# Attention backward of a transformer block: dQ by 256-column matmuls over two column strips of TensorE in place of 128-column matmuls over four

## The chip, the cores and the metric

The kernel runs on one core of a Trainium2 chip. The metric is the device time of one execution in microseconds (us), lower is better. Within the core the engines work side by side and meet at semaphores: TensorE (PE, with PEld for its weight loads), VectorE (DVE), ScalarE (ACT), GpSimd (POOL) and SyncE (SP), which issues most of the DMAs.

## What is computed

The reference is one block with adaptive layer norm: x + ga * attention(h1), then x + gb * mlp(h2), and its vector-Jacobian product for all inputs. There are 2048 tokens, width 512, 32 heads of 16 columns. The change lies in the gradient of the attention:

```python
qkv = (x @ wqkv).reshape(B, S, 3, H, Dh)          # H = 32, Dh = 16
scores = einsum('bhqd,bhkd->bhqk', q, k) * scale  # scale = Dh ** -0.5
p = softmax(scores)
o = einsum('bhqk,bhkd->bhqd', p, v)
# backward: P = exp(scores) normalized, dP = dO V^T - rowsum, dS = P * dP
# dQ = scale * dS K,  dK = scale * dS^T Q,  dV = P^T dO
```

Weights and activations are bf16 and sums are kept in float32.

## The kernel before

The kernel is a sequence of stages: QKV and the forward attention with the MLP woven in, the MLP's backward, the attention's backward (`attn_bwd`, from some 1184 to 2414 us of the profile), and the gradients of the QKV projection. In the attention's backward the order on PE and SP is the program order (`manual_schedule`), and in the forward part and the last stage too; ScalarE's, VectorE's and GpSimd's orders follow from it.

`attn_bwd` loops over 8 groups `g` of four heads, two pairs `jp` of heads in each, 4 blocks `c` of 512 keys, and 16 blocks `ib` of 128 queries taken in fours (`ib0`, `i`). One pass of the innermost loop handles 128 queries, 512 keys and two heads `a`. 8 x 2 x 4 x 16 makes 1024 passes. In a pass:

- For each head, PE multiplies Q by K into a tile `st` of PSUM (L1584; three such buffers), then ScalarE takes the exponential into `pu` (L1587).
- Between the two, PE makes dP of the pass before into `dp` (L1509; three buffers), and VectorE multiplies it with `pu` into `ds` (L1513). S uses one half of the array's rows and dP the other. In one pass of eight (`off`) the second of these products is made by GpSimd (L1522), from a copy that ScalarE makes (L1521).
- After an odd pass, `kv_two` calls `kv` for two older query blocks: 4 matmuls each (L1455), 512 columns over four strips of 32 columns of the array, that add dK and dV into `acckv`. When all queries of a key block are done, ScalarE copies it to `kvT` (L1458).
- After an even pass, four units of `dq` (eight if many are queued) add dQ into `accq` (L1478). A unit is one head `a`, one 128-key part `sub` of the key block and the four query blocks of an `ib0`. Its operand `dsT` holds the transposed `ds`.
- In pass `i == 2` a DMA or, for a part in every second four, PE transposes `ds` into `dsT` (`turn_ds`, L1543, and ScalarE's copy L1544). The DMA is issued on SP at the end of the four (`dS`, L1530), into one of four `dsT` buffers.
- After all key blocks of a pair, VectorE scales `accq` into `dqT` (L1483). `turn_q` transposes this on PE (L1491) and ScalarE writes the token-major result `dq_t` (L1492). For dK and dV `turn` does the same (L1468, L1472). Turns are taken from a queue at `i == 1`, which is directly after the dQ matmuls of the pass before.

`accq` is one bank of PSUM (128 partitions x 512 float32). Before the change its partition strip is the query block within the four, `i`, and its column block is `b = ib0 // 4`.

Of the kernel before, what the change touches and what calls it, by code (L numbers as in the profile page):

```python
# [10 lines left out]
F32 = mybir.dt.float32  # L11
ACT = mybir.ActivationFunctionType
ALU = mybir.AluOpType
# [6 lines left out]
P = 128  # L20
DH = 16
# [84 lines left out]
class K:  # L106
# [1322 lines left out]
    def attn_bwd(self):  # L1429
# [7 lines left out]
        tc, nc = self.tc, self.nc  # L1437
        S, D, H, NQ, ST, SC = self.S, self.D, self.H, self.NQ, self.ST, self.SC
        G = 4
        W = 4 * DH  # L1440
        dtp, kvp, stp, dpp = self.dtp, self.kvp, self.stp, self.dpp
        accp = self.accp
        acckv = accp.tile([P, 512], F32, name="acckv")
        nc.vector.memset(acckv[:], 0.0)
        accq = accp.tile([P, ST // G, P], F32, name="accq")
        masked, kvs = self.masked, self.kvs
        pend, pendq, turnq = [], [], []

# [11 lines left out]
        def turn(g, jp, kvT, s0):  # L1460

            if kvT is None:
                return turn_q(g, jp)
            h0 = 4 * g + 2 * jp
            n = ST // 2
            tp = stp.tile([P, n, P], BF16, name="st")
            for st in range(n):
                nc.tensor.transpose(tp[:, st, :], kvT[:, (s0 + st) * P:(s0 + st + 1) * P], self.ident[:])  # L1468
            v = tp[:].rearrange("p s (t a e) -> p t s a e", t=2, a=2)
            for t, dst in enumerate((self.dk_t, self.dv_t)):  # L1470
                d = dst[:, s0:s0 + n, h0 * DH:(h0 + 2) * DH].rearrange("p s (a d) -> p s a d", a=2)
                nc.scalar.copy(d, v[:, t, :, :, 0:DH])  # L1472

        def dq(u):
            (T, g, jp, c, ib0, a, sub, dsT) = u
            col = 32 * (2 * jp + a) - DH * a
            for i in range(G):
                nc.tensor.matmul(accq[32 * i:32 * i + 32, ib0 // G, :], lhsT=T["K"][:, 4 * c + sub, col:col + 32],  # L1478
                                 rhs=dsT[:, (i * 2 + a) * 4 + sub, :],
                                 start=(c == 0 and ib0 == 0 and a == 0 and sub == 0), stop=False,  # L1480
                                 skip_group_check=True)
            if (c, ib0, a, sub) == (SC - 1, ST - G, 1, 3):
                nc.vector.tensor_scalar(self.dqT[:], accq[:].rearrange("p b q -> p (b q)"), self.scale, None, ALU.mult)  # L1483
                turnq.append((g, jp, None, 0))

        def turn_q(g, jp):

            h0 = 4 * g + 2 * jp
            tp = stp.tile([P, ST // G, P], BF16, name="st")
            for b in range(ST // G):  # L1490
                nc.tensor.transpose(tp[:, b, :], self.dqT[:, b * P:(b + 1) * P], self.ident[:])  # L1491
            nc.scalar.copy(self.dq_t[:, :, h0 * DH:(h0 + 2) * DH], tp[:].rearrange("p b (i e) -> p (b i) e", i=G))  # L1492

        def kv_two(n=2):
            for u in pend[2 - n:2]:
# [51 lines left out]
        T = self.T0  # L1547
        last = None
        for g in range(NQ):
            for jp in range(2):  # L1550
# [15 lines left out]
                for c in range(SC):  # L1566
                    c0 = 512 * c
                    for ib0 in range(0, ST, G):
# [6 lines left out]
                        for i in range(G):  # L1575
                            ib = ib0 + i
                            q = slice(ib * P, (ib + 1) * P)
                            if turnq and i == 1:
                                turn(*turnq.pop(0))
                            pu = self.pup.tile([P, 2, 512], BF16, name="pu")  # L1580
                            for a in range(2):
                                stt = stp.tile([P, 512], F32, name="st")
                                rs = slice(64 * jp, 64 * jp + 64)
                                nc.tensor.matmul(stt[:], lhsT=T["QT"][rs, q], rhs=masked["KT"][a][rs, c0:c0 + 512],  # L1584
                                                 start=True, stop=True)
                                held = dP(last, a) if last else None
                                nc.scalar.activation(pu[:, a, :], stt[:], ACT.Exp, scale=self.scale)  # L1587
                                if held is not None:
                                    dP_pool(last, held)
                            if last:  # L1590
                                dS(last)
                            last = (T, g, jp, c, ib, kvT, pu, dsg, i, grp)
                            if i % 2 == 1 and len(pend) >= 4:
                                kv_two()
                            elif i % 2 == 0 and len(pendq) > 4 * G:
                                for _ in range(8 if len(pendq) > 6 * G else 4):
                                    dq(pendq.pop(0))
                            if i == 2:
                                turn_ds(dsg, grp, off(c, ib))
            T = Tn  # L1600
        with tc.manual_schedule(engines=ALL):
            for t in (2, 0):
                for p in self.wq_pieces(t):
                    nc.gpsimd.dma_start(*p)
            for a in range(2):
                dP(last, a)
            dS(last)
            while len(pend) > 2:
                kv_two()
            kv(pend[0])  # L1610
            for _ in range(2 * G):
                dq(pendq.pop(0))
            kv_two(1)
            k0, v0, k1 = [dpp.tile([P, 512], F32, name="dp") for _ in range(3)]
            self.dw_mm(k0, 1, 0, 0, ST // 2)
            turn(*turnq.pop(0))
            for _ in range(2 * G):
                dq(pendq.pop(0))
            self.dw_mm(v0, 2, 0, 0, ST // 2)
            self.dw_mm(k0, 1, 0, ST // 2, ST)  # L1620
            self.col_sum(1)
            self.dw_mm(v0, 2, 0, ST // 2, ST)
            self.col_sum(2)
            self.cs_bc(1)
            while pendq:
                dq(pendq.pop(0))
            self.cs_bc(2)
            turn(*turnq.pop(0))
            self.dw_mm(k1, 1, 1, 0, ST)
# [312 lines left out]
```

## Time and profile before

| what | value |
|---|---|
| median of 3 runs | 2524.97 us (2520.79 to 2530.05) |
| profiled execution | 2524.31 us, its span 2522.4 us |
| granted TensorE clock | 0.998 |
| dQ matmuls (L1478) | 8192, 128 x 32 weights, 128 columns, median 219 ns each as recorded |
| dK and dV matmuls (L1455) | 4096, 128 x 16 weights, 512 columns, 381 ns each |
| S (L1584) and dP (L1509) matmuls | 2048 each, 512 columns, 381 and 382 ns |
| exponentials (L1587) | 2048, 641 ns each |
| products ds (L1513) | 1920, 681 ns each |
| transposes of ds by DMA (L1530) | 256, median 7.1 us from issue to landing |

A matmul's recorded duration is its way through the array and is longer than the time until the next may start, so starts must be compared, not durations. The same holds for ACTIVATE and TENSOR_TENSOR: one starts before the record of the one before it ends. In a line of groups the columns are the line of the code, the engine, the operation, what it writes and reads, shape, count, busy time and mean. In the timeline they are the start, the length of the merged group, engine, line, operation and count.

### The profile page before, as it was taken

Reading aid. Unit: us, or ns where it says so; the run is one execution under the profiler, and the core shown is the slowest. Engines: PE = TensorE matmul, PEld = TensorE weight load, DVE = VectorE, ACT = ScalarE, POOL = GpSimd, SP = SyncE. Lnnn points to the kernel's source line nnn. Section 1 sums busy time; section 2 is a strip of 40 time slices with the busy share of each in tenths; the row PEclk is TensorE's granted clock in tenths of the full one; section 3 lists DMA queues with packets and bytes.
Section 4 is the critical chain, followed back from the end, with each engine's and each line's share of the span. In section 5 each row is a group of like instructions: output and inputs, shape, how many; then the busy total and the mean of one; then the engine's idle time right before and its main releaser. Section 6 shows DMA issues by size and latency. Waiting matters only on the chain.

```text
span 2522.4 us, 76903 instructions
## 1 busy us (share of the span) xinstructions
PE 2433.1 (96%) x30791; PEld 1107.9 (44%) x30791; DVE 1705.4 (68%) x3519; ACT 2296.2 (91%) x3773; POOL 713.9 (28%) x1289
## 2 busy tenths in 40 slices
PE   8999999999999999989999999999999999999998
PEld 4555555555555554673333333333333333333343
DVE  6222223422332343667999999999999999999957
ACT  7999999999999997535999999999999999999945
POOL 2344531321131022255222222222222222222223
PEclk9999999999999999999999999999999999999999
DMA  4589761441343044699999999999999999999997
GB/s 167 134 178 202 179 114 64 116 99 44 103 118 74 24 137 129 139 191 214 234 221 218 218 226 220 223 227 218 219 218 223 225 221 221 222 228 226 237 211 198
DMA packets 1260558, 446.30 MB, mean 177 GB/s; under 512 B 1204052, under 2 KB 1228246, under 8 KB 1260198
## 3 DMA queue, kind: packets, MB, share of 16 engines
q1 hardware_dynamic: 1219654, 336.29, 70.7%
q0 software_dynamic: 38464, 104.04, 13.9%
q8 instruction: 241, 3.95, 0.7%
q10 hardware_dynamic: 2080, 1.05, 0.1%
q14 instruction: 119, 0.97, 0.1%
HBM read 75.83 MB, written 64.49 MB: 56 GB/s over the span
## 4 chain that ended last, share of the span: by engine, by line
PE 59%; ACT 22%; DMA 11%; issue 4%; DVE 3%; SPq 1%; POOL 0%; DVEq 0%; ACTq 0%; POOLq 0%
ACT pu L391 18%; PE st L1584 17%; DMA dsT<-ds 8%; PE acckv L1455 8%; PE st L388 8%; PE accq L1478 5%; PE accbank L322 3%; PE dp L1509 3%; ACT pu L1587 2%; PE dps L1050 2%; PE pps L1237 2%; PE dps L995 1%; DVE ds L1513 1%; PE st L1543 1%; PE pps L631 1%
## 5 line engine op out<-in xcount | busy, mean ns | idle before, releaser
L1513 DVE TENSOR_TENSOR ds<-dp,pu 128x512 bf16<-128x512 f32 x1920 | 1178.3, 681 | 44.5 <-PE dp L1509 26.4
L1587 ACT ACTIVATE pu<-st 128x512 bf16<-128x512 f32 x2048 | 1073.9, 641 | 39.4 <-PE st L1584 21.3
L391 ACT ACTIVATE pu<-st 128x1024 bf16<-128x1024 f32 x992 | 912.2, 1077 | 5.4 <-PE st L388 5.1
L388 PE MATMUL st<-QTm,KTq 128*128 128x512 bf16 x1984 | 588.4, 377 | 19.7 <-ACT pu L391 6.1
L322 PEld LDWEIGHTS <-pu 128*128 128x128 bf16 x8192 | 347.2, 96 | 236.2 <-issue 3.2
L322 PE MATMUL accbank<-Vaug,pu 128*128 128x17 bf16 x8192 | 357.6, 171 | 1.2 <-ACT Vaug L522 0.9
L1509 PE MATMUL dp<-kvm,q 64*128 64x512 bf16 x1024 | 356.4, 382 | 2.2 <-DVE g2w L1056 0.7
L1509 PE MATMUL dp<-kvm,dOTg 64*128 64x512 bf16 x1024 | 356.2, 382 | 0.9
L1584 PE MATMUL st<-kvm,QTg 64*128 64x512 bf16 x1024 | 327.2, 381 | 10.5 <-ACT pu L1587 7.4
L1584 PE MATMUL st<-kvm,q 64*128 64x512 bf16 x1024 | 326.6, 380 | 10.8 <-ACT pu L1587 7.6
L388 PEld LDWEIGHTS <-KTq 128*128 128x128 bf16 x1984 | 188.2, 96 | 177.5 <-issue 125.9
L1522 POOL TENSOR_TENSOR ds<-junk,pu 128x512 bf16<-128x512 f32 x64 | 73.7, 1151 | 378.6 <-DVE ds L1513 336.7
L1522 POOL TENSOR_TENSOR ds<-csq,pu 128x512 bf16<-128x512 f32 x64 | 73.8, 1154 | 356.6 <-ACT csq L1521 356.6
L302 POOL DMA_DIRECT2D QTm<-QTq_d x124 | 63.5, 514 | 342.7 <-PE st L388 321.3
L1455 PE MATMUL acckv<-ds,Qg 128*16 128x512 bf16 x1024 | 154.3, 381 | 0.0
L1455 PE MATMUL acckv<-pu,dOg 128*16 128x512 bf16 x1024 | 154.2, 381 | 0.0
L1455 PE MATMUL acckv<-pu,q 128*16 128x512 bf16 x1024 | 154.0, 381 | 0.0
L1455 PE MATMUL acckv<-ds,q 128*16 128x512 bf16 x1024 | 154.0, 381 | 0.0
L329 DVE RECIPROCAL rl<-accbank 128x4 f32<-128x4 f32 x128 | 22.9, 179 | 159.5 <-PE accbank L322 159.2
L1584 PEld LDWEIGHTS <-q 64*128 64x128 bf16 x1024 | 58.1, 94 | 137.9 <-issue 104.5
L1584 PEld LDWEIGHTS <-QTg 64*128 64x128 bf16 x1024 | 57.7, 94 | 137.7 <-issue 102.7
L1509 PEld LDWEIGHTS <-q 64*128 64x128 bf16 x1024 | 88.4, 93 | 64.2 <-issue 47.4
(387 smaller groups left out, 3138.6 us busy)
## 6 DMA issues: line engine op xcount, KB each, us to landing
KTq<-KTq_d POOLq DMA_DIRECT2D x24, 512.0 KB, 3.8
duT_d<-auT POOLq DMA_DIRECT2D x3, 1792.0 KB, 8.2
aT_d<-rT POOLq DMA_DIRECT2D x3, 1792.0 KB, 11.6
KTq_d<-KTq SPq DMA_DIRECT2D x32, 128.0 KB, 2.0
QTq_d<-ev_fm SPq DMA_DIRECT2D x32, 128.0 KB, 3.4
ktm_d<-ev_tm POOLq DMA_DIRECT2D x32, 128.0 KB, 2.5
VTq_d<-vT POOLq DMA_DIRECT2D x4, 1024.0 KB, 5.8
dsT<-ds SPq DMA_TRANSPOSE x256, 7.1
```

Source lines behind the costliest of these rows:

```text
L302: nc.gpsimd.dma_start(QTm[j][32 * j:32 * j + 32, :], self.QTq_d[g, 32 * j:32 * j + 32, 512 * qc:512 * (qc + 1)])
L322: nc.tensor.matmul(acc[:, a, sub, :], lhsT=pu[:, a, sub * P:(sub + 1) * P], rhs=Vaug[:, kb, h, :], start=(kb == 0 and a == 0 and sub == 0) ...
L388: nc.tensor.matmul(stt[:, a, :], lhsT=KT[:, kb * P:(kb + 1) * P], rhs=QTm[2 * jp + a][:], start=True, stop=True)
L391: nc.scalar.activation(pu[:], stt[:], ACT.Exp, scale=self.scale)
L1050: nc.tensor.matmul(pt[:], lhsT=a[st], rhs=g_tm[:, st, :], start=(st == 0), stop=(st == ST - 1))
L1455: nc.tensor.matmul(acckv[r:r + DH, :], lhsT=T[n][:, ib, col:col + DH], rhs=src[:, a, :], start=(ib == 0), stop=(ib == ST - 1))
L1478: nc.tensor.matmul(accq[32 * i:32 * i + 32, ib0 // G, :], lhsT=T["K"][:, 4 * c + sub, col:col + 32], rhs=dsT[:, (i * 2 + a) * 4 + sub, :], ...
L1509: nc.tensor.matmul(dp[:], lhsT=T["dOT"][rd, ib * P:(ib + 1) * P], rhs=masked["VT"][a][rd, 512 * c:512 * (c + 1)], start=True, stop=True)
L1513: nc.vector.tensor_tensor(dsg[:, i, a], dp[:], pu[:, a, :], ALU.mult)
L1522: nc.gpsimd.tensor_tensor(dsg[:, i, 1], f[:], pu[:, 1, :], ALU.mult)
L1584: nc.tensor.matmul(stt[:], lhsT=T["QT"][rs, q], rhs=masked["KT"][a][rs, c0:c0 + 512], start=True, stop=True)
L1587: nc.scalar.activation(pu[:, a, :], stt[:], ACT.Exp, scale=self.scale)
```

## The change

A unit of `dq` issues two matmuls of 256 columns in place of four of 128. `h` picks two neighbouring query blocks of the four; they lie 8 blocks of 128 apart in `dsT`, so the moving operand has two runs of 128 columns. Each `h` has a strip of 32 array columns of its own, strips 0 and 1 for even `b`, 2 and 3 for odd `b`, and half of the bank's columns. The sum lands in another place of `accq`, so `turn_q`'s copy is written as two copies of half the width, which undo it. The transposes between, the scaling and all loads stay.

```diff
-        accq = accp.tile([P, ST // G, P], F32, name="accq")
+        accq = accp.tile([P, 512], F32, name="accq")
...
-            for i in range(G):
-                nc.tensor.matmul(accq[32 * i:32 * i + 32, ib0 // G, :], lhsT=T["K"][:, 4 * c + sub, col:col + 32],
-                                 rhs=dsT[:, (i * 2 + a) * 4 + sub, :],
-                                 start=(c == 0 and ib0 == 0 and a == 0 and sub == 0), stop=False,
+            b = ib0 // G
+            for h in range(2):
+                r, o = 32 * (2 * (b % 2) + h), 256 * (b // 2)
+                nc.tensor.matmul(accq[r:r + 32, o:o + 256], lhsT=T["K"][:, 4 * c + sub, col:col + 32],
+                                 rhs=dsT[:].rearrange("p (i w) k -> p i w k", i=G)[:, 2 * h:2 * h + 2, 4 * a + sub, :],
+                                 start=(c == 0 and b < 2 and a == 0 and sub == 0), stop=False,
                                  skip_group_check=True)
...
-                nc.vector.tensor_scalar(self.dqT[:], accq[:].rearrange("p b q -> p (b q)"), self.scale, None, ALU.mult)
+                nc.vector.tensor_scalar(self.dqT[:], accq[:], self.scale, None, ALU.mult)
...
-            nc.scalar.copy(self.dq_t[:, :, h0 * DH:(h0 + 2) * DH], tp[:].rearrange("p b (i e) -> p (b i) e", i=G))
+            for h in range(2):
+                nc.scalar.copy(self.dq_t[:, 8 * h:8 * h + 8, h0 * DH:(h0 + 2) * DH].rearrange("p (s i) e -> p s i e", i=2),
+                               tp[:, 2 * h:2 * h + 2, :].rearrange("p i (s e) -> p s i e", s=G))
```

## The prediction, made before the changed kernel was run

> **What bounds the kernel now.** I read the page's parts 1 and 4 first, then the busy times by stage, then TensorE's timeline inside the changed stage. The page says that PE and ScalarE are both near full over the span, and that the chain that ended last is mostly PE's:
>
> ```profile
> PE 2433.1 (96%) x30791; PEld 1107.9 (44%) x30791; DVE 1705.4 (68%) x3519; ACT 2296.2 (91%) x3773; POOL 713.9 (28%) x1289
> ...
> PE 59%; ACT 22%; DMA 11%; issue 4%; DVE 3%; SPq 1%; POOL 0%; DVEq 0%; ACTq 0%; POOLq 0%
> ```
>
> The changed matmuls (L1478) run from 1183.9 to 2414 us. Busy times by stage (the second line is the attention backward; columns are length, PE, PEld, DVE, ACT, POOL, clock, DMA):
>
> ```profile
> 0.00:1184.00 1184.00, 1142.53 (x13162) 645.06 (x13166) 450.40 (x1400) 1046.78 (x1246) 362.81 (x596) 1.00 0.53 127
> 1184.00:2414.00 1230.00, 1192.95 (x17184) 419.57 (x17187) 1173.43 (x1915) 1196.49 (x2423) 316.78 (x633) 1.00 1.17 223
> ```
>
> In that stage PE, VectorE and ScalarE are all 95 to 97% busy, so no one busy share names the bound. PE's timeline shows who waits:
>
> ```profile
> 1606.91 0.39 PE L1584 MATMUL st<-kvm,q 64*128 64x512 bf16 x1
> 1606.91 0.39 PE L1509 MATMUL dp<-kvm,q 64*128 64x512 bf16 x1
> 1607.14 0.38 PE L1584 MATMUL st<-kvm,q 64*128 64x512 bf16 x1
> 1607.14 0.38 PE L1509 MATMUL dp<-kvm,q 64*128 64x512 bf16 x1
> 1607.45 0.41 PE L1478 MATMUL accq<-dsT,keep 128*32 128x128 bf16 x16
> 1607.79 0.39 PE L1584 MATMUL st<-kvm,q 64*128 64x512 bf16 x1
> 1607.79 0.39 PE L1509 MATMUL dp<-kvm,q 64*128 64x512 bf16 x1
> 1608.01 0.38 PE L1584 MATMUL st<-kvm,q 64*128 64x512 bf16 x1
> 1608.30 0.37 PE L1509 MATMUL dp<-kvm,q 64*128 64x512 bf16 x1
> 1608.60 0.39 PE L1455 MATMUL acckv<-ds,q 128*16 128x512 bf16 x2
> ```
>
> I call one pass over a query block a step: S0, P0, S1, P1 (scores L1584, and dP L1509 of the step before), then a burst: dQ (16 matmuls) in even steps, dK/dV (L1455, 8 matmuls) in odd ones. Where nothing waits, S and P start together (1607.14). At 1608.30 P1 starts 0.29 us after its S1: it waits for a dp bank that VectorE (L1513) still reads. So PE, although "busy", waits here.
>
> The start stamps of the trace give the sums. Over the 1230 us, PE's shortest steps are 226+3+303+339 = 871 ns with a dQ burst and 226+3+303+541 = 1073 with a dK/dV burst; 512 of each are 995 us, 128 blocks of transposes (L1543, 329 ns) 42, and 48 turns (L1468, L1491, 330 to 550) some 24: 1061. VectorE starts a tile every 598 ns when fed: 1920 + 16 are 1158. ScalarE: 2048 x 477, 256 copies x 465, 64 x 569, 64 x 262, 16 x 482 are 1157. Hence VectorE and ScalarE set the pace, PE has 169 us of waits, and the 72 us above 1158 are starts that VectorE missed.
>
> **What the Trainium skill says.** "TensorE: Matmul & The Clock Gate", section on the back-to-back issue gap, gives 134 cycles at 128 columns and 262 at 256, at 2.4 GHz 56 and 109 ns. The trace agrees for the first: groups of four dQ matmuls start 56 ns apart. The 256 is in no trace yet; 512 columns (L1455) repeat after 219. The same page, on packing small matmuls, says that matmuls in different column groups overlap with starts about 4 ns apart; here 2 to 3 ns. Its section on LDWEIGHTS prices a load by its columns, P/1.2: an estimate of 27 ns for 32. In the trace these loads are issued ahead and hide. "TensorEngine Tiling (Array Packing)", key properties, says that a change of tiling mode drains the array. The trace agrees: from the last dQ start to the next S 148 ns pass, not 56. The change keeps 128x32 tiles and the number of switches.
>
> **The change part by part.** All times below stand against the profiled execution, 2524.31 us (span 2522.4, 1.9 around it), 0.03% under the median 2524.97.
>
> Burst. A unit was four matmuls of 128 columns over four strips, 56 ns. It becomes two of 256 over two strips; four units in a row have the same block of queries, so they use the same two strips, and the other two stand idle. A unit takes 109 ns. Four units: 3 x 53 more between starts, 53 more in the last, some 6 less for fewer starts: 339 becomes 543, +204. The dK/dV burst is the check: 2 x 512 columns, as many as 4 x 256, take 541. Ends: with one load of 27 ns exposed per unit, +312; if instructions rather than columns cost, -112 (rival 3). I take +205. 512 bursts make 105 us on PE, whose sum becomes 1166: level with VectorE's 1158, and no more than 8 us above. What the end sees is how much of each 205 PE's lead covers.
>
> Regular steps. VectorE starts tile n at 598n; a dp bank can be rewritten 728 ns after that start, and a P reaches VectorE 524 after its own start (smallest stamps). So P1 waits until 468 before its step's first tile; the next P0 comes one burst later and is needed 1196-524 after that tile. Lead: 1140-642 = 498 behind a dQ burst, now 293; 296 behind dK/dV, unchanged. Still positive: no cost. Without that cover each burst would cost 205.
>
> The eight steps that repeat. Step 2 adds transposes behind the burst: 642+329 = 971, lead 169; now 1176, VectorE idles 37. In step 6 a product goes to POOL instead (L1521, L1522), so VectorE needs the next tile 598 earlier: P1 at 728 after an earlier tile, burst, P0, 524: 728+642+524 = 1894 against 1794, idle 100; then the step behind it 202. Measured medians are 105 and 189, so the method holds. After: 728+848+524 = 2100, idle 306, and the second idle falls to 0, since VectorE is late already. Sum 302 before, 343 after: +41 per eight steps, x128 = 5.2 us.
>
> kvT copies (L1458, 569 ns on ScalarE, in 62 of those eights, behind step 3). Count from VectorE's start on the first tile of step 2; there P1 is at -468. Now the last transpose starts at -468+642+177 = 351; the dsT copy (L1544) follows 255 later at 606, two exps from 1071, the kvT copy at 2025, the next exp at 2594. Its bank is free 670 later, at 3264, and S1 of step 5, due at 2792, waits 472 (measured 506). P1 behind it is at 3270, two bursts later a tile reaches VectorE at 5515 where 5382 was due: 133 idle instead of 100, and the second idle is as much shorter: nothing lost. After: transpose 555, copy 810, exps 1275, kvT copy 2229, exp 2798, S1 at 3468, the next P0 at 3474+847 = 4321, reaching VectorE at 4845 (24 idle), the one behind the longer burst at 5399+524 = 5923 against 5443: 480 idle. 504 in place of 306: 198, x 62 = 12.3 us (ends 0, if ScalarE catches up sooner, and 15).
>
> Turns (32 of kvT, 16 of dqT) stand directly behind a dQ burst. They already outrun the lead of 498; with 293 each costs 205 more, and some 50 at the next transposes: 48 x 255 = 12.2 us (ends 0 and 15).
>
> DMA waits before dQ: 22, 13.8 us in all. Each finds up to 205 less lead: 0 to 4.5, I take 2. Tail: 24 units that only PE works on, x 53 = 1.3. The dqT evacuation (L1483) reads the same 512 columns, and VectorE reaches it about a microsecond later than PE, so 205 stay hidden. The two half copies that replace L1492 are like L1472, 2 x 262 for 482: 0.7 us on ScalarE in all, hidden behind VectorE, 0.7 if not. A dsT buffer comes free 205 later, one of four: nothing. The strided two-block operand is read at one column a cycle: nothing.
>
> Sum 5.2+12.3+12.2+2+1.3 = 33 us: 2557.
>
> **Rivals.** 1, all on the path: PE becomes the bound with its present waits kept, 512 x 205 + 1.3 = 106, 2630. For it: the chain in this stage is PE throughout, and the three sums become equal, so each stall of one stalls all. Against: 169 us are 165 ns of waits per step, and leads that stay positive.
> 2, absorbed: PE's 169 us of waits swallow it except the tail and the step sum; 1 to 9 us, 2526 to 2533. For it: VectorE's and ScalarE's sums are untouched. Against: waits aren't where turns and kvT copies need them.
> 3, faster: dQ is bound by the issue of pairs of load and matmul, 14 ns each. Two pairs make 28 ns a unit, the burst falls to 227, leads grow by 112. The 302 idle per eight steps lose some 224 (29 us), the turns 5: 2490. It decides if units start less than 56 ns apart. Against: four starts follow within 10 ns and then 46 pass, and L1455 with the same instructions takes 219.
> That instructions are not halved is excluded: the order of PE has 8192 rows fewer, 2 x 4096.
>
> **How the numbers follow.** About 0.3% (8 us) can be told from no change. Forecast (2533 to 2585) 0.66; rival 1, in part or whole (2585 to 2635) 0.15; rival 2 0.13; rival 3 0.06. Faster 0.05 (rival 3, less its weak end), same 0.11, slower 0.84. The range 2530 to 2595 leaves out rival 3, part of 2 and the upper part of 1.
>
> **What would show it.** Right: L1478 x4096 of 128x256, units 109 ns apart, bursts near 543; VectorE's idle up by about 33 us in this stage, at step 6 and behind turns; PE's waits per step down from 165 to some 95 (1263 less 1166 us, by 1024). Wrong: bursts shorter than 339, or VectorE's idle unchanged, or waits of P for a bank as frequent as now.

## The result and the profile after

The changed kernel takes 2553.16 us (median of 5 runs, 2549.51 to 2553.91) against 2524.97 us: 28 us slower, a ratio of 1.011 with a 95% interval of 1.0093 to 1.0126. The forecast was 2557 us, in 2530 to 2595. The profiled execution took 2553.91 us, its span 2552.0.

The page after, first and fourth part:

```profile
PE 2476.8 (97%) x26695; PEld 1131.4 (44%) x26695; DVE 1717.6 (67%) x3519; ACT 2315.0 (91%) x3789; POOL 715.9 (28%) x1289
...
PE 62%; ACT 20%; DMA 9%; issue 5%; DVE 3%; POOL 1%; SPq 0%; DVEq 0%; POOLq 0%; ACTq 0%
```

There are 4096 matmuls fewer, and PE is busy for 44 us more. Busy times by stage (columns as before; the attention's backward now ends some 26 us later, so the window is longer):

```profile
0.00:1184.00 1184.00, 1143.01 (x13154) 645.86 (x13154) 456.79 (x1400) 1046.58 (x1246) 364.06 (x596) 1.00 0.53 127
1184.00:2440.00 1256.00, 1232.92 (x13058) 440.68 (x13057) 1179.29 (x1915) 1214.55 (x2437) 317.51 (x633) 1.00 1.11 218
```

Up to 1184 us nothing of weight has changed. By the start stamps, from the first score matmul to the last dP the stage takes 1259.3 us in place of 1231.0, and what follows it 123.3 in place of 122.2. All of the difference is in the changed loop and its tail.

PE's timeline in the loop after the change:

```profile
1608.31 0.39 PE L1588 MATMUL st<-kvm,q 64*128 64x512 bf16 x1
1608.31 0.39 PE L1513 MATMUL dp<-kvm,q 64*128 64x512 bf16 x1
1608.53 0.38 PE L1588 MATMUL st<-kvm,q 64*128 64x512 bf16 x1
1608.54 0.38 PE L1513 MATMUL dp<-kvm,q 64*128 64x512 bf16 x1
1608.84 0.61 PE L1480 MATMUL accq<-dsT,keep 128*32 128x256 bf16 x8
1609.39 0.39 PE L1588 MATMUL st<-kvm,q 64*128 64x512 bf16 x1
1609.39 0.39 PE L1513 MATMUL dp<-kvm,q 64*128 64x512 bf16 x1
1610.02 0.37 PE L1588 MATMUL st<-kvm,q 64*128 64x512 bf16 x1 [0.25 <-ACT pu L1591]
```

Eight dQ matmuls stand where there were sixteen, and the next score matmul follows 0.55 us after the first of them (1608.84 to 1609.39), where it followed after 0.34. Over all bursts the median is 546 ns; the forecast had 543. In the last line, S1 of a step behind a kvT copy, a score matmul waits for ScalarE.

VectorE shows where the time goes. Its timeline before, from 1700 us on; one row is a run of tiles without a gap of note, and the bracket is the gap ahead of it with what ended it:

```profile
1699.32 7.37 DVE L1513 TENSOR_TENSOR ds<-dp,pu 128x512 bf16<-128x512 f32 x12
1706.99 6.09 DVE L1513 TENSOR_TENSOR ds<-dp,pu 128x512 bf16<-128x512 f32 x10 [0.29 <-PE dp L1509]
1713.36 1.96 DVE L1513 TENSOR_TENSOR ds<-dp,pu 128x512 bf16<-128x512 f32 x3 [0.28 <-ACT pu L1587]
```

The same after:

```profile
1700.43 9.19 DVE L1517 TENSOR_TENSOR ds<-dp,pu 128x512 bf16<-128x512 f32 x15 [0.23 <-PE dp L1513]
1710.00 9.17 DVE L1517 TENSOR_TENSOR ds<-dp,pu 128x512 bf16<-128x512 f32 x15 [0.39 <-ACT pu L1591]
1719.41 7.73 DVE L1517 TENSOR_TENSOR ds<-dp,pu 128x512 bf16<-128x512 f32 x12 [0.23 <-PE dp L1513]
```

A gap now comes once in 15 tiles, which is once in eight steps: behind step 6, whose second product GpSimd makes. Shorter waits are hidden within a row: 15 tiles that start 598 ns apart, the last of 681 ns, would fill 9.05 us, and the rows take 9.19 and 9.17; 12 would fill 7.26, and the last row takes 7.73. VectorE's waits in the stage, before and then after (total us, times, longest):

```profile
DVE ds L1513 <- PE dp L1509: 26.2, 61, 2.0
...
DVE ds L1513 <- ACT pu L1587: 3.1, 11, 0.3
```

```profile
DVE ds L1517 <- ACT pu L1591: 30.3, 85, 0.4
DVE ds L1517 <- PE dp L1513: 29.2, 81, 3.0
```

A row in a timeline or in the waits counts a gap between records. The start stamps count more finely: I call idle what lies between two starts of VectorE's tiles beyond 598 ns, the spacing without a wait. Summed over the run, by the step whose first tile comes late (us; e1 to e9 are experiments below):

| ahead of | before | after | e8: long bursts in steps 0, 4 | e9: in steps 2, 6 | e3 | e1 |
|---|---|---|---|---|---|---|
| step 3 (behind transposes) | 9.3 | 15.1 | 9.4 | 15.0 | 16.9 | 62.0 |
| step 5 (behind turns) | 8.5 | 10.6 | 11.7 | 8.7 | 15.6 | 49.1 |
| step 6 | 0.8 | 3.1 | 0.6 | 3.7 | 2.8 | 0.0 |
| step 7 (behind GpSimd's product) | 19.4 | 49.1 | 20.3 | 49.8 | 51.0 | 94.3 |
| step 0 | 21.5 | 2.7 | 21.1 | 2.7 | 2.5 | 1.0 |
| step 1 (behind turns and waits of dQ for dsT) | 19.0 | 24.6 | 36.4 | 16.7 | 42.1 | 48.7 |
| all | 82.3 | 110.7 | 103.8 | 100.3 | 135.9 | 260.6 |

The rows leave out the second tiles of a step and steps 2 and 4 (3.8 us before, 5.5 after). Ahead of step 3 some 9 us in each column aren't idle: 15 times VectorE evacuates `accq` there (L1483), which takes one tile's time. So the transposes cost 0.4 us before and 6.1 after.

The sum grows by 28.4 us, the stage by 28.3. That the two agree is arithmetic, since VectorE starts as many tiles as before and still 598 ns apart where it doesn't wait. What the table adds is the place of the loss: behind GpSimd's product, transposes and turns, and ahead of step 1.

### The profile page after: what moved, and what is told of

The parts are those of the page before. It is cut to its first block, busy times and chain, and to the rows that moved or that the text cites. A ratio compares the mean times of both kernels' runs of the same rounds, so it can differ in the third digit from the quotient of the medians.

```text
span 2552.0 us, 68728 instructions
## 1 busy us (share of the span) xinstructions
PE 2476.8 (97%) x26695; PEld 1131.4 (44%) x26695; DVE 1717.6 (67%) x3519; ACT 2315.0 (91%) x3789; POOL 715.9 (28%) x1289
## 4 chain that ended last, share of the span: by engine, by line
PE 62%; ACT 20%; DMA 9%; issue 5%; DVE 3%; POOL 1%; SPq 0%; DVEq 0%; POOLq 0%; ACTq 0%
PE st L1588 17%; ACT pu L391 16%; PE acckv L1455 9%; PE accq L1480 8%; PE st L388 8%; DMA dsT<-ds 6%; PE accbank L322 3%; ACT pu L1591 2%; PE dp L1513 2%; PE dps L1050 2%; DVE ds L1517 2%; PE pps L1237 2%; PE st L1547 1%; PE dp L1639 1%; PE st L1734 1%
## 5 line engine op out<-in xcount | busy, mean ns | idle before, releaser
L388 PE MATMUL st<-QTm,KTq 128*128 128x512 bf16 x1984 | 588.8, 378 | 19.8 <-ACT pu L391 6.0
L1513 PE MATMUL dp<-kvm,q 64*128 64x512 bf16 x1024 | 337.6, 383 | 1.9 <-DVE g2w L1056 0.7
L1513 PE MATMUL dp<-kvm,dOTg 64*128 64x512 bf16 x1024 | 335.7, 381 | 0.9
L1588 PE MATMUL st<-kvm,q 64*128 64x512 bf16 x1024 | 321.1, 383 | 7.4 <-ACT pu L1591 5.4
L1588 PE MATMUL st<-kvm,QTg 64*128 64x512 bf16 x1024 | 320.1, 381 | 7.5 <-ACT pu L1591 5.7
L1480 PE MATMUL accq<-dsT,keep 128*32 128x256 bf16 x2048 | 157.5, 276 | 4.2 <-DMA dsT<-ds 3.7
L1480 PE MATMUL accq<-dsT,Kg 128*32 128x256 bf16 x2048 | 156.5, 275 | 3.6 <-DMA dsT<-ds 3.4
L1588 PEld LDWEIGHTS <-q 64*128 64x128 bf16 x1024 | 58.2, 94 | 156.3 <-issue 137.2
L1480 PEld LDWEIGHTS <-keep 128*32 128x32 bf16 x2048 | 81.6, 95 | 102.6 <-issue 97.8
```

The lines of the kernel that those rows point to most:

```text
L388: nc.tensor.matmul(stt[:, a, :], lhsT=KT[:, kb * P:(kb + 1) * P], rhs=QTm[2 * jp + a][:], start=True, stop=True)
L1480: nc.tensor.matmul(accq[r:r + 32, o:o + 256], lhsT=T["K"][:, 4 * c + sub, col:col + 32], rhs=dsT[:].rearrange("p (i w) k -> p i w k", i=G) ...
L1513: nc.tensor.matmul(dp[:], lhsT=T["dOT"][rd, ib * P:(ib + 1) * P], rhs=masked["VT"][a][rd, 512 * c:512 * (c + 1)], start=True, stop=True)
```

## Experiments

My theory: a burst costs the columns on its busiest strip, and the end sees only what PE's lead over VectorE doesn't cover (the time by which a dP reaches VectorE before it is needed). Rivals: the added array time goes straight to the end (1); slack takes it all (2); instructions cost rather than columns (3). Each ratio is to the kernel before on the same chip.

**e1, one strip.** All four query blocks in one matmul, a quarter of the instructions of before.

```diff
-            for h in range(2):
-                r, o = 32 * (2 * (b % 2) + h), 256 * (b // 2)
-                nc.tensor.matmul(accq[r:r + 32, o:o + 256], lhsT=T["K"][:, 4 * c + sub, col:col + 32],
-                                 rhs=dsT[:].rearrange("p (i w) k -> p i w k", i=G)[:, 2 * h:2 * h + 2, 4 * a + sub, :],
+            nc.tensor.matmul(accq[32 * b:32 * b + 32, :], lhsT=T["K"][:, 4 * c + sub, col:col + 32],
+                             rhs=dsT[:].rearrange("p (i w) k -> p i w k", i=G)[:, :, 4 * a + sub, :],
...
```

The copy in `turn_q` is written to match.

> One dQ matmul of 512 columns on one strip a unit, a quarter of the instructions of before. If a burst costs its columns on the busiest strip (my theory): units 216 ns apart, burst to the next score matmul 972 ns instead of 339; TensorE's sum rises from 1061 to some 1385 us and passes VectorE's 1158, the lead is gone (1140-303-972 is below zero), and the stage becomes TensorE's: 1395 to 1425 us, the run some 2690 to 2720, about 2705. If all of the added time fell on the path (rival 1): 512 x 633 ns = 324 us, 2849. If instructions cost and not columns (rival 3): a run shorter than before, 2480 or so. If slack swallowed it (rival 2): within 10 us of the change, 2565 at most.

Measured: 2705.17 us, ratio 1.0703 (1.0688 to 1.0719). PE's timeline:

```profile
1701.68 0.38 PE L1510 MATMUL dp<-kvm,dOTg 64*128 64x512 bf16 x1
1701.99 1.04 PE L1478 MATMUL accq<-dsT,keep 128*32 128x512 bf16 x4
1702.96 0.62 PE L1468 MATMUL st<-ident,kvT 128*128 128x128 bf16 x8
```

The burst, here ahead of a turn, takes 0.97 us (1701.99 to 1702.96); the median is 969 ns, and its units start 216 ns apart. The stage is now PE's:

```profile
1170.00:2579.00 1409.00, 1407.03 (x11020) 401.52 (x11018) 1203.91 (x1936) 1260.45 (x2444) 317.62 (x632) 1.00 0.95 193
```

PE is busy in 1407 of 1409 us, and the stage lies 24 us above the sum of 1385. Rivals 1 and 3 missed by over 140 us, and slack can't hold 180. The fewer the instructions, the slower: what counts is the width on one strip.

**e2, half the columns.** The changed kernel with 128 columns a matmul (and accq cleared at first). It leaves out half of the sum for dQ.

```diff
-                nc.tensor.matmul(accq[r:r + 32, o:o + 256], lhsT=T["K"][:, 4 * c + sub, col:col + 32],
-                                 rhs=dsT[:].rearrange("p (i w) k -> p i w k", i=G)[:, 2 * h:2 * h + 2, 4 * a + sub, :],
+                nc.tensor.matmul(accq[r:r + 32, o:o + 128], lhsT=T["K"][:, 4 * c + sub, col:col + 32],
+                                 rhs=dsT[:].rearrange("p (i w) k -> p i w k", i=G)[:, 2 * h, 4 * a + sub, :],
```

> The changed kernel with each dQ matmul cut to 128 columns: the same instructions and the same two strips, half the columns. It leaves out dQ of every second query block. Column theory: units 56 ns apart, burst some 335 ns, as in the kernel before, and the time of before within 5 us: 2520 to 2530. If fewer instructions are worth time by themselves (rival 3): burst near 227 ns and 2490. If the two idle strips or the two-copy turn cost, not the columns: it stays near the changed kernel, 2550.

Measured: 2519.72 us, ratio 0.9976 (0.9966 to 0.9986), burst 333 ns. With as few instructions as the changed kernel the time of before is back, even 6 us under it and just outside what was expected (2520 to 2530). VectorE's idle is 82.5 us in the profile, as before. Rival 3 had 227 ns and 2490: half the instructions are worth 6 ns of a burst and no more. Two strips by themselves cost nothing.

**e3, every unit twice.** The kernel before, 16384 dQ matmuls.

```diff
-            for i in range(G):
+            for n in range(2 * G):
+                i = n % G
...
-                nc.vector.tensor_scalar(self.dqT[:], accq[:].rearrange("p b q -> p (b q)"), self.scale, None, ALU.mult)
+                nc.vector.tensor_scalar(self.dqT[:], accq[:].rearrange("p b q -> p (b q)"), self.scale / 2, None, ALU.mult)
```

> The kernel before with each dQ unit issued twice (and half the scale): four times the instructions of the changed kernel, the old four strips, but a burst of 339 + 4 x 56 = 563 ns, 17 more than the changed kernel's 546. Column and lead theory: the same idle of VectorE at the same steps, 3 to 8 us over the changed kernel: 2556 to 2561. If the two-strip form or the operand of two runs has a cost of its own: clearly below the changed kernel, 2540 or less. If instructions cost (rival 3): far above, 2580 and more. Rival 1, all on the path: 512 x 224 = 115 us, 2640.

Measured: 2579.08 us, ratio 1.0206 (1.0189 to 1.0223); a miss, 18 us above the expected. The time alone would almost fit what was expected of rival 3, and the burst, 563 ns as expected, can't tell the two apart: 8 rounds of 56 ns are also 32 pairs of 14. What excludes rival 3 is the changed kernel's own burst, with e1, e2 and e7. Steps 3, 6, 7 and 0 lose 3 us more than in the changed kernel. The rest is ahead of steps 1 and 5, 22.5 us more than after. There dQ waits for transposed ds. Before, after, and in e3:

```profile
PE accq L1478 <- DMA dsT<-ds: 13.8, 22, 2.1
```

```profile
PE accq L1480 <- DMA dsT<-ds: 7.1, 10, 2.4
```

```profile
PE accq L1479 <- DMA dsT<-ds: 27.8, 40, 2.1
```

These waits grow by 20.7 us over the changed kernel. The transposing DMAs move the same bytes, but their 256-byte packets take 24.2 ns on average, against 22.7 before and 22.2 after, and from issue to landing a transpose takes 7.6 us in the median, against 7.1 and 6.8. So e3 is no clean measure of array time; it has a second effect, which goes through the DMAs.

**e7, each matmul in two.** Instructions of before, strips and columns of after.

```diff
-            for h in range(2):
-                r, o = 32 * (2 * (b % 2) + h), 256 * (b // 2)
-                nc.tensor.matmul(accq[r:r + 32, o:o + 256], lhsT=T["K"][:, 4 * c + sub, col:col + 32],
-                                 rhs=dsT[:].rearrange("p (i w) k -> p i w k", i=G)[:, 2 * h:2 * h + 2, 4 * a + sub, :],
+            for i in (0, 2, 1, 3):
+                r, o = 32 * (2 * (b % 2) + i // 2), 256 * (b // 2) + 128 * (i % 2)
+                nc.tensor.matmul(accq[r:r + 32, o:o + 128], lhsT=T["K"][:, 4 * c + sub, col:col + 32],
+                                 rhs=dsT[:, (i * 2 + a) * 4 + sub, :],
...
```

> The changed kernel with each matmul of 256 columns issued as two of 128 on the same strip: as many instructions as before the change (8192), the two strips of the change, so the column time of the change. Column theory: burst 546 to 556 ns and the changed kernel's time, 2553, or up to 6 us more if the instruction count acts on the transposing DMAs: then their packets go back from 22.2 to 22.7 ns and the waits for transposed ds from 10 to some 20. Rival 3 in its weak form, halving the instructions is worth array time: burst above 560 ns and 2565 or more. If spread-out instructions are harmless to the DMAs and the packets stay at 22.2, the slower packets of the doubled kernel (24.2) have another cause.

Measured: 2556.14 us, ratio 1.0128 (1.0113 to 1.0143), burst 556 ns: 3 us over the changed kernel, intervals overlapping. Idle rises by 6.6 us over the profile after, ahead of steps 1 and 3 for the most part. The packets are back at 22.8 ns, but dQ waits for dsT only 10 times, 9.8 us: only half of the second expectation came true. With columns and strips alike, twice the instructions move the time by 0.1 to 0.2%, which the intervals don't tell from nothing. A burst at 14 ns an instruction pair would have taken 339 ns (rival 3). And the operand of two runs, which e7 does without, costs nothing: the burst is 10 ns longer without it.

**e8 and e9, long bursts in half of the places.** The changed form for one head's units alone (e8: `a == 0`, steps 0 and 4; e9: `a == 1`, steps 2 and 6).

```diff
+            if a == 0:
                 for h in range(2):
...
+            else:
+                for i in range(G):
+                    nc.tensor.matmul(accq[32 * i:32 * i + 32, 128 * b:128 * b + 128], lhsT=T["K"][:, 4 * c + sub, col:col + 32],
+                                     rhs=dsT[:, (i * 2 + a) * 4 + sub, :],
...
```

> The changed form for the units of head a = 0 alone, which are issued in steps 0 and 4; a = 1 (steps 2 and 6) keeps the old form, 6144 matmuls. The sum for dQ is scattered wrongly in accq, so dQ and what follows from it is not the reference's; all work is done. Lead theory: the lead of steps 0 and 4 covers 205 ns except where a turn stands behind: 5 to 12 us over the kernel before, about 2533. Uniform cost (each burst the same share): 14 us, 2538. Rival 1: 52 us.

> The reverse: the changed form for a = 1 alone, issued in steps 2 and 6, the old one in steps 0 and 4; dQ scattered wrongly as well. Lead theory: VectorE's idle behind steps 2 and 6 as in the changed kernel (17 to 20 us), that at turns as before: 2540 to 2545. Uniform cost: 14 us, 2538. Rival 1: 52 us.

Measured: e8 2543.52 us, 1.0079 (1.0066 to 1.0093), 18 us over before; e9 2541.79 us, 1.0067 (1.0054 to 1.0080), 16 us. Rival 1 is out for both. VectorE's timeline in e8, and then in e9:

```profile
1711.42 6.30 DVE L1525 TENSOR_TENSOR ds<-dp,pu 128x512 bf16<-128x512 f32 x10 [0.29 <-PE dp L1521]
1718.01 1.95 DVE L1525 TENSOR_TENSOR ds<-dp,pu 128x512 bf16<-128x512 f32 x3 [0.28 <-ACT pu L1599]
```

```profile
1703.94 9.12 DVE L1525 TENSOR_TENSOR ds<-dp,pu 128x512 bf16<-128x512 f32 x15 [0.39 <-ACT pu L1599]
1713.29 7.53 DVE L1525 TENSOR_TENSOR ds<-dp,pu 128x512 bf16<-128x512 f32 x12 [0.23 <-PE dp L1521]
```

e9 has the gaps of the changed kernel, e8 those of before: in the table, steps 3, 7 and 0 of e9 equal after to 0.7 us, so the transposes, GpSimd's product and the kvT copies were placed rightly. By the times alone a uniform cost, 14 us for each, would fit about as well; the places of the idle speak against it, and e5 and e6 below. But e8 costs more than its 5 to 12 us, most of it ahead of step 1 (19.0 to 36.4). Sorting its 125 eights (runs of eight steps): where a turn stands behind step 0 the idle goes from 9.5 to 12.7 us, where dQ waits for dsT from 8.7 to 13.4, and in the 86 others, where the forecast saw a lead of 498 ns and no cost, from 0.2 to 10.0. The two halves add to 34 us, the whole change is 28: they aren't independent. The last part says why, for the 86 and for the turns.

**e5 and e6, no product for GpSimd.** In the kernel before (e5) and the changed one (e6) the same lines are left out:

```diff
-            if a == 1 and i == 1 and off(c, ib):
-                return dp
             nc.vector.tensor_tensor(dsg[:, i, a], dp[:], pu[:, a, :], ALU.mult)
```

> The kernel before with no product given to GpSimd: VectorE makes all 2048, 1225 + 10 us of starts, so it is the slowest engine by far and no step asks for a tile 598 ns early. Lead theory: the 41 us of idle behind step 6 vanish, those of turns stay; stage some 1255 to 1270 us against 1231, run 2550 to 2565. If TensorE were the bound of the stage as the chain of waits has it, taking work from ScalarE and giving it to VectorE would leave the time where it is, 2525.

> The changed kernel with no product given to GpSimd. Lead theory: with VectorE ahead as the bound the longer bursts cost only at transposes (some 37 to 55 ns, 128 times: 5 to 7 us) and turns (8 us), 10 to 17 us over the kernel before in the same form instead of 28. If each burst's 205 ns went straight to the end (rival 1), or cost a fixed share wherever they fall: 28 us or more over that form.

Measured: e5 2560.09 us, 1.0143 (1.0126 to 1.016); e6 2567.93 us, 1.0167 (1.0149 to 1.0185). The change costs 8 us here instead of 28, less even than expected. PE does exactly the same matmuls in both pairs; what differs is that VectorE makes 128 tiles more and ScalarE 128 copies fewer. Ahead of steps 7 and 0, where the idle was 40.9 us before and 51.8 after, it is 0.1 us in both. This tells most sharply that the added 105 us of array time have no price of their own. It also shows that the chain of waits, PE throughout, doesn't name the bound: with 128 tiles more on VectorE the time rose by 36 us.

**e4 and e10, turns without a burst ahead of them.** The kernel before, in search of a faster version: a dQ burst is left out when a turn waits, and made up two steps later.

```diff
-                            elif i % 2 == 0 and len(pendq) > 4 * G:
-                                for _ in range(8 if len(pendq) > 6 * G else 4):
+                            elif i % 2 == 0 and len(pendq) > 4 * G and not (i == 0 and turnq):
+                                for _ in range(8 if len(pendq) > (5 if i else 6) * G else 4):
```

e10 adds `and (c * SC + ib0 // G) % 2 == 0` within the bracket, so that it touches step 0 alone.

> The kernel before, but when a turn is waiting the dQ burst ahead of it is left out and made up two steps later by one of eight units (563 ns). If turns cost because they stand behind a burst that has used the lead up: the gap ahead of the score matmul falls from about 1209 to some 870, VectorE's idle of 27 us at steps 1 and 5 falls by 10 to 18, against 5 back at the longer bursts behind: 2510 to 2520. If those idle times come from the waits for transposed ds or from ScalarE's copies instead: no change or up to 5 us slower.

> As the kernel with turns alone, but only for turns at step 1; those at step 5 stay behind their dQ burst, since the burst that made up for them fell on step 6, where it cost VectorE 4 us. Step 1 gains 6 us as there, the longer burst at step 2 costs 55 ns 15 times, 1 us: 2520, 5 us under the kernel before. If the gain of 3.5 us there had another cause than the place of the turns: 2522 to 2526.

Measured: e4 2522.21 us, 0.9982 (0.9969 to 0.9996); e10 2523.57 us, 0.9989 (0.9979 to 0.9999). In e4 the idle ahead of step 1 falls from 19.0 to 13.3 us, and ahead of step 7 it grows from 19.4 to 26.9, since the burst of eight falls on step 6; step 0 gives 3.9 back. In e10 step 1 falls only to 16.9. Both missed what was expected, 2510 to 2520 and 2520, and e10 lies where it would if the gain had another cause. Both are below the time of before by less than 0.2%. The idle ahead of step 1 moves with the place of the turns, but the time hardly does, and no version here is clearly faster than the kernel before.

**e11 and e12, both kernels again**, for the packets.

> The kernel before, unchanged, for its DMA packets: if the mean 22.7 ns of a 256-byte transposing packet belongs to the form of the dQ matmuls it comes again, within 0.1; if it changes from run to run it may lie anywhere from 22.1 to 23.1. Time 2520 to 2530.

> The changed kernel, unchanged, likewise: 22.2 ns again if it belongs to the form, and 10 waits for transposed ds; otherwise anywhere from 22.1 to 23.1. Time 2549 to 2554.

Measured: e11 2526.52 us and 22.6 ns, e12 2558.03 us (one run, 4 us over the expected) and 22.2 ns with 12 waits for dsT. In one more run of each, the packets' duration came again within 0.1 ns, so it looks like the kernel's and not the run's.

## Why the prediction was right, step by step

- **Burst.** 543 forecast, 546 measured, with units 109 ns apart as forecast; e1 (969 against 972) and e2 (333 against 335) confirm the rule of columns per strip for a quarter and for half of the instructions. One reading was a little off: starts within a unit lie 3 to 4 ns apart, not 2 to 3.
- **Regular steps.** "Still positive: no cost" holds for step 4: where no turn and no wait for dsT comes between, the median lead there was 392 ns before and is 148 after. It fails for step 0: 76 before, -46 after. This step of the forecast was wrong. It took the lead of an undisturbed stretch, 498 ns, for both, and at step 0 four things eat into it:
  - The next P0 reaches VectorE 620 ns after its start, not 524, in all 71 of 97 such eights after in which VectorE waits ahead of step 1.
  - P1 of step 7 waits for VectorE, because GpSimd makes a product of step 6, and a dK/dV burst follows. So P1 of step 0 starts at best 298 ns before its step's first tile, not 468. In 38 of 88 eights before that is all, and their lead was 235 (498 - 96 - 170 = 232).
  - In 57 eights after, 41 of them behind a kvT copy, S1 of step 0 is late as well: it follows its S0 by 406 ns, where 226 is enough. It starts 705 behind the first exp of step 7, whose bank it takes over, and this exp stands 465 behind ScalarE's copy for GpSimd. Their lead is -46, and they idle 3.5 us in all.
  - At the first step of a pair of heads, S of the new pair and dP of the old one use the same half of the array's rows. There they run one after the other, P0 227 ns behind S0 in place of 3. The lead was -12 and is -218, 3.3 us of idle in 15 eights.

The third of these in the changed kernel, ScalarE's copy and exps, then S0 and S1 of step 0:

```profile
1709.79 0.62 ACT L1525 COPY junk<-dp 128x512 f32<-128x512 f32 x1
1710.25 4.16 ACT L1591 ACTIVATE pu<-st 128x512 bf16<-128x512 f32 x8
1710.55 0.39 PE L1588 MATMUL st<-kvm,QTg 64*128 64x512 bf16 x1
1710.96 0.37 PE L1588 MATMUL st<-kvm,QTg 64*128 64x512 bf16 x1
```

e5 and e6 test this. Without GpSimd's product and ScalarE's copy for it, P1 of step 0 starts 465 ns before the tile and the lead behind step 0 is 396 in e5; in e6 only the first steps of a pair still idle there, 1.8 us. Less small gains at other steps it is 5.4 us that the forecast had at 0.

- **Transposes.** 37 x 128 = 4.7 us forecast; 5.8 measured.
- **Step 6 and kvT copies.** 306 idle and then 0 in eights without a kvT copy; measured 311 and 43. In those with one, 480 and 24; measured 459, and 49 ahead of step 6. Together 12.8 forecast (41 - 37 = 4 ns by 128, and 12.3), 13.2 measured over steps 6, 7 and 0.
- **Turns.** This term was mis-sized: 12.2 us forecast, 3.5 measured (16.3 to 19.8 us over the 46 turns in the loop). The forecast had every turn beyond the lead already, so that each cost 205 ns more, and 50 at the next transposes. Three things were otherwise, by medians of VectorE's idle behind a turn:
  - The 15 turns of dQ had not used the lead up. They went from 0 to 142 ns.
  - The 16 turns of dK and dV at step 5 went from 360 to 475. Before, the score matmul behind them waited for a bank that ScalarE had not emptied: from the first transpose to that matmul 766 ns passed, and 635 after. The longer burst took up part of this wait.
  - The 15 turns of dK and dV at step 1 went from 619 to 664. In these eights VectorE is already later: ahead of steps 7 and 0 it idles 484 ns, where it was 277 + 36. In e8, which leaves steps 7 and 0 as before, the same turns cost 825, which is 206 more than before, as forecast.

  The 50 at the next transposes didn't show: ahead of step 3 behind a turn at step 1 VectorE doesn't idle at all.
- **Waits for dsT.** 2 us forecast, -0.6 measured: the waits halved, as shown under e3.
- **Tail.** 1.3 us forecast, 1.1 measured.

So the mechanism stands: columns on the busiest strip make the burst, and the end sees what the lead doesn't cover. But two terms were off in opposite ways, -8.7 and +5.4 us, and that the sum of 33 came so near to 28 is in part luck. The rivals: all on the path would have been 106 us, and e1, e5 and e6 exclude it; absorbed would have been 9 at most; the gain from fewer instructions is excluded by e2 for the array. Its weak form remains: fewer dQ instructions mostly go with faster DMAs.

## What to carry over

The dQ matmuls on different 32-column strips ran side by side here, so a burst's price was the number of columns on the busiest strip (56 ns a unit for 128, 109 for 256, 216 for 512), not the total of columns, and hardly the number of instructions (546 or 556 ns a burst for 8 or 16 matmuls). Halving the instructions by doubling the width on half of the strips nearly doubled what a unit takes. In a loop that three engines nearly fill, price such a change at the places where the next engine has no lead (irregular steps, turns, an offloaded product). Check for every one of these whether a third engine, here ScalarE, is already late there, and whether the engine behind is late itself, so that a delay costs less. The sum of an engine's work tells how near the bound is; it doesn't tell what a longer burst costs, which here was 28 us of 105, and 8 of 105 when VectorE had more to do.

## What was not expected of the hardware

The 256-byte packets of the DMA transposes take a mean time that goes with the dQ matmuls. The figures of 22.7, 22.2 and 24.2 ns above are means over a whole run (1,175,574 packets in every kernel), of which some 977,000 fall between the first and the last dQ matmul. For these alone the mean is 20.6 ns with 2048 matmuls (e1, whose stage is also longer), 21.6 to 21.9 with 4096 (after, e2, e6, e12), 22.2 to 22.8 with 8192 (before, e4, e5, e7, e10, e11) and 24.2 with 16384 (e3). Columns aren't the cause (after and e2), nor strips (after and e7). But e8 and e9 have 6144 each and show 22.3 and 21.6, so the count alone isn't it either; when the bursts fall against the DMAs may matter. What the instructions and the DMAs share here is open; no run told it apart.
